# A transformer block on one core: the second MLP product copies its first results and adds the residual on GpSimd

## The chip, the cores and the metric

One core of a Trainium2 chip. Its engines run side by side, each with its own queue: TensorE (PE, matrix products, results in PSUM banks), VectorE (DVE), ScalarE (ACT), GpSimd (POOL) and SyncE (SP), which here only issues DMAs. The metric is the device time of one execution in microseconds (us). Before the change: 2175.38 us, the median of 3 runs (2174.56 to 2177.39).

## The reference

In float32, 2048 tokens of 1024 values, 32 heads of 32, 3584 hidden values:

```
h  = x + attention(layernorm(x)) @ wo            # 4 segments of 512 tokens with a running memory
y  = layernorm(layernorm(h))
g  = gelu(y @ w1 + b1)                           # 2048 x 3584
h2 = h + (g @ w2 + b2)                           # 2048 x 1024, the output
```

## The kernel before

Every float32 product is made of three matmuls: each operand is split into a rounded high half and a low half that holds the rest (ACT casts the high half, DVE or GpSimd subtracts to get the low one), and high x high, high x low, low x high are summed in one bank.

The program runs over two halves of 1024 tokens. A half has attention (16 units of a head group and a segment, a table of steps gives the order), the product with `wo`, and the first MLP product in 14 pairs of column blocks (`Mixer.pair`), which makes `gelu` and stores it to DRAM (`h_dram`). Near the end of half 0, beside the last nine pairs, `ln1` normalises the next half's tokens: `ln_transpose` (L156) turns 128 x 128 blocks on PE into a bank of the tags it is given, ACT and DVE take them out as halves. The pairs take their own banks by tags: `bps` from `d` (three banks), `dps` from `pt` (two). The tags `qk` (two) belong to attention's scores.

After half 1 comes the second MLP product, class `Second`, by Strassen's seven products in Winograd's form. `Second` runs 112 jobs, two rounds (s = 0 and 1, one for each half of the hidden values) of 56. A round goes through the product names 1, 7, 6, 5, 3, 2, 4; a job is a name and a pair p of token tiles p and p + 8 (8 pairs); 1 alternates with 7, 6 with 5, 3 with 2. A job is 21 matmuls: 7 blocks of 128 by three. In round 1, job 56 is the first, job 70 is (7, pair 6), job 72 is (6, pair 0), job 73 (6, pair 1), job 75 (6, pair 2). What stands around a job n is in `work(n)`, called after the matmuls of n are written down, and each engine runs its part in that order:

- `rows_ahead`, `load_rows` (L1264): SP loads rows of `w2` or stored sums of them (`w2r`, four buffers) a few jobs ahead
- `load_items` (L1311, L1308): SP loads items, 128 x 896 tiles of `gelu` (`hr`), into one of six buffers, first freed, first used, up to six jobs ahead, and no further than buffers are free
- `sums` (L1331 to L1344): GpSimd combines items. For name 6 the sum of L1336 and L1337 needs three items; the second sum is also stored to DRAM (`s2_dram`, L1402) in the next job's `work`, to be loaded again for name 3
- `prep` (L1357, L1358): ACT casts and DVE subtracts the item of job n + 2. It stands two jobs ahead of its use, on three buffers in turn. When it is done the item's buffer is free again
- `add` (L1428): DVE adds the bank to one or two of the 32 output tiles `c` (128 x 512, all kept in SBUF)
- `fill` (L1275, L1283, L1284): GpSimd pre-sums two rows of `w2`, ACT and DVE make halves of them
- `ahead`: `out` gives a home to the output tiles that the next two jobs need and loads the residual `h` + b2 into them from `h1_dram` (L1372), so that every `add` adds to the residual. The 32 loads lie between the end of the pairs and job 13

SP issues in the written order; a load that waits for its buffer holds all behind it. At most eight of SP's DMAs are under way: each has one of eight queue semaphores in turn and waits for the DMA that had it before.

## Time and profile before

| | us |
|---|---|
| median of 3 runs | 2175.38 |
| profiled execution, its time | 2176.5 |
| profiled execution, its span | 2174.8 |
| PE busy in the span | 2154.5 |
| DVE, ACT, POOL busy | 1357.8, 1100.5, 950.1 |
| second MLP product: from about 1636 to the end, PE busy there | 532.99 of 538.80 |

Rows of the profile name line, engine, operation and tile. In the list of waits a row gives the engine and its line, what ended the wait, the sum, the number and the longest. In a timeline a row gives start, length, engine, line, operation, and in brackets the idle time before it and what ended that. A group's row ends in count, busy us, mean ns, and the idle time before. A DMA row ends in count, size and the median us from issue to landing. GB/s and the DMA share are of 16 engines. The granted TensorE clock was 1.00 throughout the second product but for its last slice (0.98).

### The profile page before, as it was taken

How to read it: one execution, taken by the hardware profiler on the slowest of the kernel's cores; microseconds unless marked ns; L12 is line 12 of the kernel's file. 1: busy time of each engine (PE TensorE's matmuls, PEld its weight loads, DVE VectorE, ACT ScalarE, POOL GpSimd, SP SyncE). 2: the span in 40 equal slices, each digit the busy share in tenths (PEclk: the TensorE clock that was granted, in tenths of full speed). 3: DMA queues.
4: the chain of work that ended last, by engine and by line, in shares of the span. 5: the costliest groups of instructions: out<-in, count | busy, mean ns of one | idle time of the engine just before them, and what ended most of it. 6: DMA issues, size and time to landing. Idle time of an engine off the chain costs nothing.

```text
span 2174.8 us, 33225 instructions
## 1 busy us (share of the span) xinstructions
PE 2154.5 (99%) x10937; PEld 1750.0 (80%) x10937; DVE 1357.8 (62%) x2696; ACT 1100.5 (51%) x2433; POOL 950.1 (44%) x1206
## 2 busy tenths in 40 slices
PE   8999999999999999999999999999999999999999
PEld 6877777778888888877777778888888788888887
DVE  7766666655745656666667655745666665576753
ACT  5777777753543445777777753633343232322321
POOL 5533335461434434533335551534446544255340
PEclk9999999999999999999999999999999999999999
DMA  7444444664575555444444763576569865676762
GB/s 202 117 117 107 107 107 127 198 203 155 169 211 154 180 163 152 121 117 107 107 107 125 204 214 134 170 213 174 160 202 380 280 223 178 201 241 214 260 227 91
DMA packets 352405, 376.20 MB, mean 173 GB/s; under 512 B 27214, under 2 KB 244330, under 8 KB 352234
## 3 DMA queue, kind: packets, MB, share of 16 engines
q1 hardware_dynamic: 289306, 337.25, 51.3%
q10 hardware_dynamic: 62928, 36.84, 5.7%
q8 instruction: 87, 1.43, 0.3%
q14 instruction: 84, 0.69, 0.1%
HBM read 241.27 MB, written 82.38 MB: 149 GB/s over the span
## 4 chain that ended last, share of the span: by engine, by line
PE 95%; DVE 2%; ACT 1%; DMA 1%; POOL 1%; issue 0%; SPq 0%; ACTq 0%; DVEq 0%; POOLq 0%
PE po L1418 24%; PE bps L1021 11%; PE cps L1021 7%; PE dps L1021 7%; PE pst L620 4%; PE po L634 3%; PE pqk L570 3%; PE pwo L127 3%; PE vps L127 3%; PE pwo L129 3%; PE qps L127 3%; PE pwo L128 3%; PE kps L127 3%; PE qps L128 3%; PE qps L129 3%; PE vps L128 3%
## 5 line engine op out<-in xcount | busy, mean ns | idle before, releaser
L572 DVE CUSTOM_DVE_ANT_0 pqk<-pqk,mask 128x512 f32<-128x512 f32 (+2 forms) x384 | 216.9, 565 | 235.5 <-PE pqk L570 205.1
L574 ACT ACTIVATE junk<-pqk,mx 128x512 f32<-128x512 f32 (+2 forms) x384 | 225.1, 586 | 133.0 <-DVE mx L572 124.7
L627 POOL TENSOR_SCALAR_AFFINE_SELECT e<-e 128x128 f32<-128x128 f32 (+1 forms) x384 | 136.0, 357 | 259.0 <-ACT e L623 253.9
L700 POOL TENSOR_TENSOR wl<-wr,wh 128x256 fp32r<-128x256 f32 x268 | 200.6, 764 | 107.2 <-DVE wh L696 43.5
L623 ACT ACTIVATE e<-pst 128x384 f32<-128x384 f32 (+1 forms) x384 | 200.4, 528 | 67.4 <-PE pst L620 66.4
L1428 DVE TENSOR_TENSOR c<-c,po 128x512 f32<-128x512 f32 x160 | 105.4, 683 | 150.7 <-PE po L1418 143.4
L620 PE MATMUL pst<-qs,ks 104*128 104x512 f32 (+3 forms) x512 | 140.7, 318 | 2.2 <-ACT e L623 1.2
L570 PE MATMUL pqk<-ks,qs 96*128 96x512 f32 (+2 forms) x384 | 137.8, 359 | 0.9 <-ACT junk L574 0.6
L620 PEld LDWEIGHTS pst<-qs,ks 104*128 104x128 f32 x512 | 95.7, 188 | 36.1 <-ACT e L623 11.5
L1418 PE MATMUL po<-w2h,zh 128*128 128x512 f32 x378 | 121.0, 390 | 2.0 <-ACT zh L1357 1.6
L1275 POOL TENSOR_TENSOR w2r<-w2r 128x512 f32<-128x512 f32 x54 | 83.0, 1547 | 70.9 <-DMA w2r<-in_B_w 65.0
L127 PE MATMUL qps<-yh,wh 128*128 128x512 f32 x256 | 113.1, 442 | 0.0
L127 PE MATMUL kps<-yh,wh 128*128 128x512 f32 (+1 forms) x264 | 113.0, 428 | 0.0
L1021 PE MATMUL bps<-zh,sb 128*128 128x512 f32 x336 | 111.0, 391 | 0.0
L1021 PE MATMUL bps<-zh,sa 128*128 128x512 f32 x336 | 110.8, 390 | 0.0
L1134 POOL TENSOR_TENSOR s<-r 128x512 f32<-128x512 f32 x28 | 44.0, 1571 | 142.3 <-DVE sa L1150 84.8
L127 PE MATMUL vps<-yh,wh 128*128 128x512 f32 x256 | 105.0, 410 | 0.0
L1418 PE MATMUL po<-w2h,hl 128*128 128x512 f32 x322 | 103.1, 390 | 0.0
L128 PE MATMUL kps<-yl,wh 128*128 128x512 f32 (+1 forms) x264 | 102.4, 388 | 0.6 <-DVE yl L165 0.3
L129 PE MATMUL kps<-yh,wl 128*128 128x512 f32 (+1 forms) x264 | 101.8, 386 | 0.0
L128 PE MATMUL qps<-yl,wh 128*128 128x512 f32 x256 | 101.0, 395 | 0.0
L128 PE MATMUL vps<-yl,wh 128*128 128x512 f32 x256 | 100.9, 394 | 0.0
(271 smaller groups left out, 6206.7 us busy)
## 6 DMA issues: line engine op xcount, KB each, us to landing
hr<-h_dram SPq DMA_DIRECT2D x112, 448.0 KB, 5.5
w2r<-in_B_w SPq DMA_DIRECT2D x122, 256.0 KB, 4.6
r<-in_B_w SPq DMA_DIRECT2D x56, 512.0 KB, 4.3
ks<-kk SPq DMA_DIRECT2D x360, 64.0 KB, 2.0
qs<-qq SPq DMA_DIRECT2D x360, 64.0 KB, 2.0
h_dram<-ht ACTq DMA_DIRECT2D x83, 256.0 KB, 3.8
wx<-in_B_w SPq DMA_DIRECT2D x56, 256.0 KB, 3.7
o_dram<-side SPq DMA_DIRECT2D x52, 256.0 KB, 4.3
```

Source lines behind the costliest of these rows:

```text
L127: nc.tensor.matmul(ps, ah, bh, start=first, stop=False)
L128: nc.tensor.matmul(ps, ah, bl, start=False, stop=False)
L129: acts["mm"] = nc.tensor.matmul(ps, al, bh, start=False, stop=last)
L570: nc.tensor.matmul(ps, u["qs"][0:96, j, i * P:(i + 1) * P], u["ks"][0:96, j, 0:n], start=True, stop=True)
L572: nc.vector.tensor_tensor_reduce(out=ps, in0=ps, in1=mask[:, 512 - n:512], op0=ALU.add, op1=ALU.min, scale=-SCALE, scalar=3.0e38, accum_out=m)
L574: at(now[0] + 1, lambda: nc.scalar.activation(acts["junk"][:, :n], ps, AF.Exp, bias=m, scale=-1.0, accum_out=u["mx"][:, 1, i, j:j + 1]))
L620: nc.tensor.matmul(ps[:, o:o + 512 - P * jk], u["ks"][:, j, jk * P:(jk + 1) * P], u["qs"][:, j, jk * P:512], start=True, stop=True)
L623: nc.scalar.activation(e, ps[:, :w], AF.Exp, scale=SCALE)
L627: nc.gpsimd.affine_select(d, d, pattern=[[0, 2], [1, P]] if n == 2 else [[1, P]], compare_op=ALU.is_ge, fill=0.0, base=0, channel_multipli ...
L700: nc.gpsimd.tensor_tensor(l[:, c], wr[:, c], raw(h)[:, c], op=ALU.subtract)
L1021: nc.tensor.matmul(ps, x_[:, c, :], y_[:, c, :], start=first and c == 0 and n == 0, stop=last and c == 3 and n == 2, skip_group_check=True)
L1418: nc.tensor.matmul(ps, x_[:, k], y_[k], start=opens and k == 0 and i == 0, stop=closes and k == self.KP - 1 and i == 2, skip_group_check=True)
```

## The change

1. `add`: the first product that meets an output tile is copied into it (`tensor_copy`); later ones are added as before. The residual loads between the end of the pairs and job 13, `ahead` and `NEED` are gone.
2. `residual`, in jobs 34 to 67 (`LATE`): each job loads one residual tile into a buffer that is lent by the item loads, and in the next job GpSimd adds it to its output tile. `plan` gives every output tile a job in which no product is added to it for six jobs. Two of the six item buffers are lent, from job 32 on, and given back at job 68.
3. `prep` and `work`: the buffer of a sum that has yet to be stored is free only when the store has been written down (`cool`).
4. `ln1(1, 0)` beside the pairs takes its banks from the tag `qk` alone, and no more from `av`, `pt`, `pt`.
5. The load of `wv` for the next head group stands at step 13 of a unit and no more at 18 (units 2, 3, 12, 13, 14 of each half).

```diff
@@ -211,7 +211,7 @@
         l = apool.tile([P, DC, 512], F32R, tag=f"al{n}", name=f"{what}l{n}")
         return h, l
 
-    def ln1(half, sl, delay=0, aside=None, gap=1):
+    def ln1(half, sl, delay=0, aside=None, gap=1, tags=("av", "pt", "pt")):
         xs = []
         for t in range(4):
             xt = lnp.tile([P, D], F32, tag="ln", name="xt", bufs=4)
@@ -227,7 +227,7 @@
             return acts["y", sl]
 
         yield from ln_tiles(lnp, xs, None, None, False, act=True, aside=aside, gap=gap,
-                            fold=lambda src, t4: ln_transpose(src, *home(), t4, ("av", "pt", "pt"), slow=True))
+                            fold=lambda src, t4: ln_transpose(src, *home(), t4, tags, slow=True))
 
     def opening():
 
@@ -725,7 +725,7 @@
             b = 24 * n
             if n < 15 and ORDER[n + 1][0] != g:
                 g1 = ORDER[n + 1][0]
-                for name, m, m1 in (("k", 2, 9 if n > 1 else 11), ("q", 7, 17), ("v", 18 if n > 1 else 11, 25)) if n else \
+                for name, m, m1 in (("k", 2, 9 if n > 1 else 11), ("q", 7, 17), ("v", 13 if n > 1 else 11, 25)) if n else \
                         (("k", 4 if half else 14, 19), ("q", 8 if half else 17, 24), ("v", 20, 34)):
                     if name != "v" or not early:
                         at(b + m, partial(wload, g1, name))
@@ -1238,6 +1238,8 @@
             self.free = list(range(6))
             self.part, self.later = [], []
             self.c, self.np, self.came = {}, 0, {}
+            self.adds, self.lent, self.saving, self.cool = [], [], [], []
+            self.plan()
 
 
         def slot(self, q):
@@ -1358,7 +1360,10 @@
                 getattr(nc, lower).tensor_tensor(l, src, raw(h), op=ALU.subtract)
                 self.hl[n] = [x.rearrange("p (k n) -> p k n", n=P) for x in (h, l)]
                 if (s, name, p, "21") not in self.raws:
-                    self.free.append(b)
+                    if name == "6" and any(x is src for _, x in self.later + self.saving):
+                        self.cool.append((src, b))
+                    else:
+                        self.free.append(b)
 
 
         HOMES = [("sp", "c", 4)] * 4 + [("cx", "c", 3)] * 3 + [("cl", "r", 4)] * 4 + [("mq", "p1", 3)] * 3 + \
@@ -1369,28 +1374,49 @@
                 pool, tag, bufs = self.HOMES[len(self.c)]
                 pool = self.mq if pool == "mq" else acts[pool]
                 self.c[t, c] = pool.tile([P, 512], F32, tag=tag, name="c", bufs=bufs)
-                nc.sync.dma_start(self.c[t, c], h1_dram[t][:, c * 512:(c + 1) * 512])
             return self.c[t, c]
 
-        NEED = {"1": ("11", "12"), "7": ("21", "22")}
         ADDS = {"1": ("11", "12"), "7": ("21", "22"), "6": ("21",), "5": ("12", "22"), "3": ("12",), "2": ("11",), "4": ("21",)}
+        LATE = (34, 68)
         LAST = {"5": "22", "3": "12", "2": "11", "4": "21"}
 
         def at(self, p, w):
             return p + self.PAIRS * (int(w[0]) - 1), int(w[1]) - 1
 
-        def ahead(self, n):
-
-            for m in (n + 1, n + 2):
-                if m < len(self.jobs) and self.jobs[m][0] == 0:
-                    _, name, p = self.jobs[m]
-                    for w in self.NEED.get(name, ()):
-                        self.out(*self.at(p, w))
+        def plan(self):
+
+            uses = {}
+            for n, (s, name, p) in enumerate(self.jobs):
+                for w in self.ADDS[name]:
+                    uses.setdefault(self.at(p, w), []).append(n)
+            self.rest, left = {}, sorted(uses, key=lambda k: uses[k][-1])
+            for n in range(*self.LATE):
+                free = [k for k in left if uses[k][0] < n and uses[k][-1] > n + 8 and not any(n <= m < n + 6 for m in uses[k])]
+                if free:
+                    self.rest[n] = free[0]
+                    left.remove(free[0])
+            assert not left
+
+        def residual(self, n):
+
+            for o, k in self.adds:
+                nc.gpsimd.tensor_tensor(o, o, k, op=ALU.add)
+            self.adds = []
+            if n in self.rest:
+                (t, c), b = self.rest[n], self.lent[n % 2]
+                k = acts["sp"].tile([P, self.KP * P], F32, tag=f"hr{b}", name="hr", bufs=1)[:, 0:512]
+                nc.sync.dma_start(k, h1_dram[t][:, c * 512:(c + 1) * 512])
+                self.adds = [(self.c[t, c], k)]
+            if n == self.LATE[1]:
+                self.free += self.lent
+                self.lent = []
 
         def work(self, n, got):
 
-            late, self.later = self.later, []
+            self.saving, self.later = self.later, []
             self.rows_ahead(n)
+            while self.LATE[0] - 3 < n < self.LATE[1] and len(self.lent) < 2 and self.free:
+                self.lent.append(self.free.pop())
             self.load_items(n)
             self.sums(n, n + 2)
             self.prep(n + 2)
@@ -1398,9 +1424,12 @@
             self.fill_up(n)
             self.sums(n, n + 4)
             self.rows_ahead(n)
-            for d, t in late:
+            for d, t in self.saving:
                 nc.sync.dma_start(d, t)
-            self.ahead(n)
+            self.free += [b for t, b in self.cool if any(t is x for _, x in self.saving)]
+            self.cool = [k for k in self.cool if not any(k[0] is x for _, x in self.saving)]
+            self.saving = []
+            self.residual(n)
 
         def product(self, n):
             s, name, p = self.jobs[n]
@@ -1424,8 +1453,12 @@
         def add(self, s, name, p, ps):
             for w in self.ADDS[name]:
                 t, c = self.at(p, w)
-                o = self.out(t, c)
-                nc.vector.tensor_tensor(o, o, ps, op=ALU.subtract if name == "4" else ALU.add)
+                if (t, c) in self.c:
+                    o = self.c[t, c]
+                    nc.vector.tensor_tensor(o, o, ps, op=ALU.subtract if name == "4" else ALU.add)
+                else:
+                    o = self.out(t, c)
+                    nc.vector.tensor_copy(o, ps)
                 if s == 1 and w in self.LAST.get(name, ""):
                     self.later.append((out[0, t * P:(t + 1) * P, c * 512:(c + 1) * 512], o))
 
@@ -1518,7 +1551,7 @@
                     pass
             acts["ahead"] = ln1(1, 1, gap=2)
             interleave(chain(*(mixer.pair(j) for j in range(HP - 9, HP))),
-                       chain(ln1(1, 0, 2), islice(acts["ahead"], 3)), 0.17)
+                       chain(ln1(1, 0, 2, tags=("qk",)), islice(acts["ahead"], 3)), 0.17)
             mp.release()
             mq.release()
             zx.release()
@@ -1545,8 +1578,6 @@
                         second.prep(n - 8, "gpsimd")
                     if (j, n) == (HP - 1, 9):
                         second.sums(0, 2)
-                    if (j, n) == (HP - 1, 12):
-                        second.ahead(-1)
             second.prep(2)
             wp.release()
             acts["cl"] = cl = tc.alloc_tile_pool(name="cl", bufs=1, reuse_waits="tile")
```

Where it moves instructions, three places are of weight. SP at jobs 68 to 73, with the items of the second round's name 6 (h_dram01 and h_dram11 are their sources; three loads make a pair's sum, w2r are weight rows). Before, from pair 1's first item on (19540, 19571, 19573); pair 0's three were loaded ahead of these rows (19464, 19466, 19505), and s2_dram0 stores its sum:

```order
L1311 DMA hr_19540<-h_dram01_152 128x896
L1311 DMA hr_19571<-h_dram11_154 128x896
L1311 DMA hr_19573<-h_dram01_152 128x896
L1402 DMA s2_dram0_80<-hr_19505 128x896
L1311 DMA hr_19602<-h_dram01_152 128x896
L1264 DMA w2r_19624<-in_B_w2 128x512 x2
L1264 DMA w2r_19627<-in_B_w2 128x512 x2
L1264 DMA w2r_19630<-in_B_w2 128x512 x2
L1311 DMA hr_19654<-h_dram11_154 128x896
L1311 DMA hr_19656<-h_dram01_152 128x896
L1264 DMA w2r_19669<-in_B_w2 128x512
L1402 DMA s2_dram1_81<-hr_19573 128x896
```

Now, from pair 1's items on (19631, 19633, 19661); pair 0's third item, 19629, is the row ahead of them:

```order
L1313 DMA hr_19631<-h_dram01_152 128x896
L1313 DMA hr_19633<-h_dram11_154 128x896
L1313 DMA hr_19661<-h_dram01_152 128x896
L1266 DMA w2r_19683<-in_B_w2 128x512 x2
L1266 DMA w2r_19686<-in_B_w2 128x512 x2
L1266 DMA w2r_19689<-in_B_w2 128x512 x2
L1313 DMA hr_19713<-h_dram01_152 128x896
L1266 DMA w2r_19728<-in_B_w2 128x512
L1428 DMA s2_dram0_80<-hr_19629 128x896
L1266 DMA w2r_19753<-in_B_w2 128x512
L1313 DMA hr_19755<-h_dram11_154 128x896
L1313 DMA hr_19757<-h_dram01_152 128x896
```

Pair 2's third item is 19656 before and 19757 now. The load of 19757 is into the buffer of 19629, behind the store of it, and waits for that store; the store itself, once ahead of the three weight rows, now stands behind them and behind one more weight load.

GpSimd at the same place (L1336, L1337 are L1338, L1339 now; L1275 is L1277). Before:

```order
L1336 TENSOR_TENSOR hr_19464<-hr_19464,hr_19466 128x896
L1337 TENSOR_TENSOR hr_19505<-hr_19464,hr_19505 128x896
L1275 TENSOR_TENSOR w2r_19496<-w2r_19496 128x512
L1275 TENSOR_TENSOR w2r_19499<-w2r_19499 128x512
L1275 TENSOR_TENSOR w2r_19502<-w2r_19502 128x512
L1336 TENSOR_TENSOR hr_19540<-hr_19540,hr_19571 128x896
L1337 TENSOR_TENSOR hr_19573<-hr_19540,hr_19573 128x896
L1275 TENSOR_TENSOR w2r_19537<-w2r_19537 128x512
L1275 TENSOR_TENSOR w2r_19624<-w2r_19624 128x512
L1275 TENSOR_TENSOR w2r_19627<-w2r_19627 128x512
L1275 TENSOR_TENSOR w2r_19630<-w2r_19630 128x512
```

Now:

```order
L1403 TENSOR_TENSOR c_17709<-c_17709,hr_19502 128x512
L1277 TENSOR_TENSOR w2r_19450<-w2r_19450 128x512
L1333 TENSOR_TENSOR hr_19525<-hr_19489,hr_19525 128x896
L1338 TENSOR_TENSOR hr_19564<-hr_19564,hr_19600 128x896
L1339 TENSOR_TENSOR hr_19629<-hr_19564,hr_19629 128x896
L1277 TENSOR_TENSOR w2r_19555<-w2r_19555 128x512
L1277 TENSOR_TENSOR w2r_19558<-w2r_19558 128x512
L1277 TENSOR_TENSOR w2r_19561<-w2r_19561 128x512
L1338 TENSOR_TENSOR hr_19631<-hr_19631,hr_19633 128x896
L1339 TENSOR_TENSOR hr_19661<-hr_19631,hr_19661 128x896
L1277 TENSOR_TENSOR w2r_19597<-w2r_19597 128x512
```

The sums of pairs 0 and 1 and the pre-sums of weights stand in the same order as before; two residual adds now go ahead of them. What is not the same is when SP loads their items: pair 0's first two in jobs 67 and 68, once both in 66, its third in 69, once in 67.

GpSimd in jobs 51 to 54, before:

```order
L1275 TENSOR_TENSOR w2r_18895<-w2r_18895 128x512
L1275 TENSOR_TENSOR w2r_18936<-w2r_18936 128x512
L1275 TENSOR_TENSOR w2r_18973<-w2r_18973 128x512
L1331 TENSOR_TENSOR hr_18922<-hr_18920,hr_18922 128x896
L1275 TENSOR_TENSOR w2r_18976<-w2r_18976 128x512
L1331 TENSOR_TENSOR hr_19001<-hr_18961,hr_19001 128x896
```

Now:

```order
L1277 TENSOR_TENSOR w2r_18905<-w2r_18905 128x512
L1403 TENSOR_TENSOR c_17335<-c_17335,hr_18951 128x512
L1277 TENSOR_TENSOR w2r_18947<-w2r_18947 128x512
L1403 TENSOR_TENSOR c_17477<-c_17477,hr_18994 128x512
L1277 TENSOR_TENSOR w2r_18987<-w2r_18987 128x512
L1333 TENSOR_TENSOR hr_19018<-hr_18975,hr_19018 128x896
L1403 TENSOR_TENSOR c_17408<-c_17408,hr_19031 128x512
L1277 TENSOR_TENSOR w2r_18990<-w2r_18990 128x512
L1403 TENSOR_TENSOR c_17554<-c_17554,hr_19067 128x512
L1333 TENSOR_TENSOR hr_19091<-hr_19055,hr_19091 128x896
```

Between two pre-sums there is now the add of a residual tile (L1403) that SP loaded at the end of the job before, behind that job's weight rows.

## The prediction, made before the changed kernel was run

> **What bounds the kernel now.** First the page's busy times, then the list of what TensorE (PE) waited for.

> ```profile
> PE 2154.5 (99%) x10937; PEld 1750.0 (80%) x10937; DVE 1357.8 (62%) x2696; ACT 1100.5 (51%) x2433; POOL 950.1 (44%) x1206
> PE pt L281 <- ACT xt L271: 8.6, 2, 8.2
> PE po L1418 <- ACT zh L1357: 1.6, 1, 1.6
> PE dps L1021 <- DVE ht L1046: 0.9, 1, 0.9
> PE po L1418 <- DVE zh L1358: 0.4, 1, 0.4
> PE pst L620 <- ACT e L623: 1.2, 3, 0.7
> ```

> PE is busy for 2154.5 of 2174.8 us. Of the rest, 8.6 us are the opening transposes, which the diff does not touch. What it can touch is 0.9 us in the pairs and 1.6 + 0.4 = 2.0 us in the second product. So an edit here can win about 2.9 us, and can lose as much as it makes PE wait: everything is read as "what is ready how long before PE wants it".

> The chain of waits shows how the 2.0 us came about (start, length in us):

> ```profile
> 1713.63 6.08 DMA hr<-h_dram
> 1719.71 1.27 POOL w2r L1275
> 1720.99 2.53 POOL hr L1336
> ...
> 1726.06 0.95 ACT zh L1357
> ...
> 1727.03 1.10 DVE zh L1358
> ```

> This is job 19: item loads on SyncE's queue (SP), a pre-sum and two sums on GpSimd (the second left out here), the cast, the subtraction. Job 75 is the same place of the second round. Two stretches by engine show what differs (PE, PEld, DVE, ACT, POOL, clock, DMA share, GB/s):

> ```profile
> 1640.00:1690.00 50.00, 49.97 (x221) 41.08 (x221) 35.91 (x41) 15.47 (x20) 28.98 (x15) 1.00 1.03 378
> 1850.00:1900.00 50.00, 50.00 (x223) 41.40 (x222) 26.96 (x32) 16.64 (x23) 10.38 (x7) 1.00 0.62 193
> ```

> The 32 residual loads of 256 KB (8.4 MB) sit in the stretch where the DMA engines are full.

> **The gains.** The copy in place of the add leaves DVE the same number of instructions on the same bank, behind the same product; it lies beside PE: 0. Without residual loads, job 19's chain should look like job 75's, which had no wait at all: I take -2.0 us (bounds -2.0 and 0, since weight rows and sums remain). In the pairs the transposes leave the two `pt` banks that `dps` turns in; the two `qk` banks are not used by anything else there. Its wait was for the bank behind L1046: -0.9 (bounds -0.9 and 0). The earlier `wv` load puts 512 KB ahead of the query copies on SP; no wait on a weight is in the list of waits, and the attention's own there are 0.7 at most (the row of L620): 0 (bounds -0.5 and +0.5). Sum of gains: -2.9.

> **The first cost: GpSimd's queue before the second round.** The 32 residuals now pass SP and GpSimd in jobs 34 to 65, one each. In order, the add of job n waits for a load that SP issues at the end of job n-1, behind that job's weight rows, and GpSimd's next pre-sum stands behind the add. Around job 52 nothing is left to spare (from the timelines of SP, POOL, ACT and DVE):

> ```profile
> 1890.93 5.44 SPq L1264 DMA_DIRECT2D w2r<-in_B_w  x4
> 1896.94 1.29 POOL L1275 TENSOR_TENSOR w2r<-w2r 128x512 f32<-128x512 f32 x1 [2.94 <-DMA w2r<-in_B_w]
> 1898.27 0.62 ACT L1283 CAST w2h<-w2r 128x512 fp32r<-128x512 f32 x1 [2.77 <-POOL w2r L1275]
> 1898.79 0.94 ACT L1357 CAST zl<-hr 128x896 fp32r<-128x896 f32 x1
> 1900.80 2.17 DVE L1358 TENSOR_TENSOR zl<-hr,zl 128x896 fp32r<-128x896 f32 x1
> 1970.65 0.39 PE L1418 MATMUL po<-w2h,zh 128*128 128x512 f32 x1
> 1975.41 0.39 PE L1418 MATMUL po<-w2h,zl 128*128 128x512 f32 x1
> w2r<-in_B_w SPq DMA_DIRECT2D x17, 256.0 KB, 3.5
> hr<-h_dram SPq DMA_DIRECT2D x11, 448.0 KB, 5.3
> ```

> PE's operands change at 1970.65 and 1975.41, the starts of jobs 70 and 71: a job is 4.76 us, so job 56 started at 1970.65 - 14 x 4.76 = 1904.0, and its third matmul, the first that reads the low half, 0.45 later. In the changed kernel the residual load stands behind the four weight loads: issued at 1890.93 + 5.44 + 0.4 = 1896.8. The last two rows are the DMA issues of 1868 to 1912, with their median to landing: 3.5 for 256 KB, 5.3 for the larger item, so it lands at 1900.3 to 1902.1. The add is not in this trace; the nearest row is the pre-sum of the same shape, 1.29 here and 1.57 in the table below: 1901.6 to 1903.7. Then the pre-sum that stood at 1896.94: to 1902.9 to 1905.2; cast 0.62; job 56's cast 0.94; its subtraction between 1.08 and 2.17: ready at 1905.6 to 1909, wanted at 1904.5. Cost 1.1 to 4.5; as jobs 55 to 57 move together I take 2.5 for them, and 0 as the low bound, if the load lands much sooner.

> **The second cost: a buffer that is still being stored.** Until job 68 two of the six item buffers are lent to the residuals, so the items of jobs 72 and on are loaded up to two jobs later. The rows of before:

> ```profile
> 1964.20 2.18 DVE L1358 TENSOR_TENSOR zh<-hr,zh 128x896 fp32r<-128x896 f32 x1
> 1967.31 0.37 SPq L1402 DMA_DIRECT2D s_dram<-hr  x1
> 1983.23 0.33 SPq L1264 DMA_DIRECT2D w2r<-in_B_w  x1
> 1988.23 2.41 POOL L1336 TENSOR_TENSOR hr<-hr 128x896 f32<-128x896 f32 x1 [0.95 <-DMA hr<-h_dram]
> 1993.84 1.09 DVE L1358 TENSOR_TENSOR hl<-hr,hl 128x896 fp32r<-128x896 f32 x1 [5.18 <-ACT hl L1357]
> L1337 POOL TENSOR_TENSOR hr<-hr 128x896 f32<-128x896 f32 x5 | 10.9, 2187 | 5.0 <-DMA hr<-h_dram 4.7
> L1275 POOL TENSOR_TENSOR w2r<-w2r 128x512 f32<-128x512 f32 x7 | 10.9, 1569 | 4.2 <-DMA w2r<-in_B_w 4.2
> L1336 POOL TENSOR_TENSOR hr<-hr 128x896 f32<-128x896 f32 x4 | 9.9, 2474 | 14.9 <-DMA hr<-h_dram 14.9
> hr<-h_dram SPq DMA_DIRECT2D x12, 448.0 KB, 5.9
> s_dram<-hr SPq DMA_DIRECT2D x4, 448.0 KB, 6.6
> ```

> Job 75 starts at 1970.65 + 5 x 4.76 = 1994.45; its low half is ready at 1993.84 + 1.09 = 1994.93, wanted at 1994.9. It was exactly in time; any delay is PE's. The sum at 1988.23 is pair 2's first; the store at 1967.31 is that of pair 0's sum, long done by then.

> In the changed order pair 0's sums stand behind the last residual add, pair 1's come behind three pre-sums, and pair 2's third item goes into the buffer of pair 0's sum, which SP must first store to DRAM. By the group means above (GpSimd, 1960 to 2010) and the medians (DMA issues, same stretch): pair 0's last item is issued at 1964.20 + 2.18 = 1966.4 (DVE reads its buffer until then) and lands 5.9 later, 1972.3; second sum to 1974.5; three pre-sums, 4.7, to 1979.2; pair 1's sums, 2.5 + 2.2, to 1983.9 (job 73's cast then ends at 1984.9, its start: nothing lost, or 1 us). The next pre-sum ends at 1985.5, cast 0.6, and DVE does job 73's subtraction, two adds and the weight subtraction by about 1988. That frees the row buffer for SP's weight load of 1983.23, and only behind it comes the store: 1988.4 instead of 1967.3. The store takes 6.6, to 1995.0; the load into the same buffer 0.4 + 5.9, to 2001.3; sum 2.2, cast 0.9, subtraction 1.1: 2005.5 against 1994.9, 10.6 us. With the quickest rows of these kinds,

> ```profile
> hr<-h_dram SPq DMA_DIRECT2D x3, 448.0 KB, 4.2
> s_dram<-hr SPq DMA_DIRECT2D x1, 448.0 KB, 5.7
> ```

> it is 1.7 + 0.9 less in the transfers and up to 2 less in GpSimd's three pre-sums and sums: 6.0. I take 8.5 (bounds 6 and 11): the wait of jobs 55 to 57 gives the loads some time that these sums do not count. From job 77 on all six buffers are back, a pair has 9.5 us and its chain takes no longer, so the loss is paid once.

> **The sum** against the profiled execution (2176.5, span 2174.8): -2.0 - 0.9 + 0 + 2.5 + 8.5 = +8.1, 2184.6. The median of the runs shown is 2175.4, 1.1 below the profiled one, so 2183.5. Its own range: from -2.9 - 0.5 + 0 + 6 = +2.6 to 0 + 0.5 + 4.5 + 11 = +16, so 2178 to 2191.

> **Rivals.** (1) The waits do not come, and the gains do: 2175.4 - 2.9 = 2172.5, not slower. Its one mechanism is job 75's store: if the load for pair 2 need not wait for it, or SP passes the weight load of 1983.23 at its old time, pair 2 is ready as before. For it: GpSimd stood idle 14.9 us before L1336 in that stretch, so there is room for sums in another place. Against: the changed program gives that load a wait on the store, and such waits are paid already, here two of up to 6.0 us (SP's waits, 1960 to 2010):

> ```profile
> SPq L1311 <- DMA s_dram<-hr: 11.8, 2, 6.0
> ```

> It decides from a store issued before about 1978: 12.9 us of store and load, 4.2 of sum, cast and subtraction end at 1994.9. (2) Only part of the delay is paid, 3 to 5 us, since the transfers find emptier queues: 2175.4 - 2.9 + 4 = 2176.5, not told from no change. For it: the DMA share is 0.62 there, not 1.03. (3) DVE becomes the bound before the second round, because GpSimd's adds hold up its two-input subtractions:

> ```profile
> 1900.00:1960.00 60.00, 60.00 (x266) 49.69 (x265) 45.47 (x46) 16.46 (x21) 30.43 (x17) 1.00 0.75 248
> 1953.57 2.12 POOL L1336 TENSOR_TENSOR hr<-hr 128x896 f32<-128x896 f32 x1 [5.18 <-DMA hr<-h_dram]
> 1953.62 3.02 DVE L1358 TENSOR_TENSOR zl<-hr,zl 128x896 fp32r<-128x896 f32 x1
> ```

> A subtraction of 1.08 took 3.02 beside a sum of 2.12 that began 0.05 before it. If each of the 12 adds from job 55 on costs DVE 1.57, it is busy 45.5 + 18.8 = 64.3 of 60 us: 4.3 more on top of the forecast, 2187.8. [...] (4) Job 19's wait stays, because GpSimd and not the DMA made it: 2185.5, inside the forecast's range; it is not counted apart.

> **How the numbers follow.** Forecast 0.62, rival 1 0.12, rival 2 0.18, rival 3 0.08. About 0.2% (4.4 us) can be told from no change here. All gains together are 2.9 + 0.5, under that, so faster gets 0.03. Slower by over 4.4: the forecast's part above +4.4, 0.55, and rival 3, 0.08: 0.63. The rest, 0.34, is no difference. The range 2174 to 2189 leaves out half of rival 1 and part of the highest cases.

> **What would show it.** Right: in the second product PE waits for the cast and subtraction of jobs 55 to 57 (1 to 4 us) and of job 75 (6 to 11), the load of pair 2's third item waits for the store of pair 0's sum, the store is issued some 20 us later than before; the wait of 0.9 at `dps` and the 2.0 at job 19 are gone. Wrong: if that load starts without a wait, if no wait over 1 us is left after job 19, or if DVE is busy throughout 1900 to 1960.

## The result, and the profile after

The changed kernel takes 2193.06 us (median of 6 runs, 2189.87 to 2193.66), the kernel before, on the same chip, 2175.77 (6 runs): ratio 1.0071, 95% interval 1.0061 to 1.0081. It is slower by 17.3 us, where +8.1 was forecast. The profiled execution took 2193.37 us, its span is 2191.3.

What PE waited for in the second product (view of waits, 1630 to 2190; line, releaser, us in total, times, longest):

```profile
PE po L1447 <- ACT hl L1359: 4.9, 1, 4.9
PE po L1447 <- ACT zh L1359: 3.2, 2, 3.1
PE po L1447 <- DVE c L1458: 1.7, 1, 1.7
PE po L1447 <- DVE zh L1360: 1.1, 3, 0.5
PE po L1447 <- DVE hl L1360: 0.8, 1, 0.8
PE po L1447 <- DVE zl L1360: 0.7, 1, 0.7
```

Before, this list held 1.6 and 0.4 us, at job 19. Those are down to 0.3 (one of the three `zh` waits), and the wait of 0.9 at `dps` is gone from the page. In their place stand 12.3 us in two groups, as PE's timeline shows (start, length, idle time before it in brackets; one wait of 0.16 us at job 73 is left out):

```profile
1900.48 0.50 PE L1447 MATMUL po<-w2h,zh 128*128 128x512 f32 x1 [3.05 <-ACT zh L1359]
1901.61 1.22 PE L1447 MATMUL po<-w2h,zh 128*128 128x512 f32 x2 [0.39 <-DVE zh L1360]
1908.84 0.73 PE L1447 MATMUL po<-zh,zl 128*128 128x512 f32 x2 [0.74 <-DVE zl L1360]
1914.72 0.50 PE L1447 MATMUL po<-zh,hl 128*128 128x512 f32 x1 [0.82 <-DVE hl L1360]
...
1992.12 0.73 PE L1447 MATMUL po<-w2h,zh 128*128 128x512 f32 x2 [0.48 <-DVE zh L1360]
1998.46 0.47 PE L1447 MATMUL po<-zh,zl 128*128 128x512 f32 x1 [1.74 <-DVE c L1458]
2008.38 0.80 PE L1447 MATMUL po<-w2h,hl 128*128 128x512 f32 x1 [4.89 <-ACT hl L1359]
```

These are jobs 55 to 57, which the prediction named, and jobs 73 to 75, of which it named job 75 (for job 73 it had "nothing lost, or 1 us"). But 12.3 us of waits, less the 1.7 won at job 19, are not 16.5, which is what the second product became longer by (first matmul of job 0 to the start of the last `add`: 536.5 us before, 553.0 after). Two stretches after the longest waits hold the rest (PE alone: stretch, length, PE busy, granted clock, DMA share, GB/s):

```profile
1897.84:1901.25 3.41, 0.73 (x2) 1.00 1.05 407
1901.25:1904.67 3.42, 3.06 (x7) 0.50 0.75 275
...
2003.64:2007.06 3.42, 0.00 (x0) 1.00 0.63 255
2007.06:2010.47 3.41, 2.08 (x4) 0.50 0.89 257
2010.47:2013.88 3.41, 3.41 (x9) 0.50 0.78 298
```

PE reads as busy there, so no list of waits shows it, but its granted clock is 0.50: 9 matmuls in the last stretch, where the job's pace at clock 1.00 (4.76 us for 21) would make 15. What that cost is estimated as half of the busy time at 0.50: 3.06 / 2 = 1.5 us in job 55, (2.08 + 3.41) / 2 = 2.75 us in job 75, which took 7.62 us, 2.86 over 4.76.

The whole account, from the starts of the first matmul of each job: what jobs took beyond 4.76 us. A wait ahead of a job's first matmul counts with the job before. (From start to start a wait took some 0.3 us more than its row says: the rows of the two groups sum to 5.0 and 7.3 us, the starts give 6.1 and 8.4, which stand in the column "waits".)

| jobs | before | after | of that, waits | of that, slow clock |
|---|---|---|---|---|
| 0, 1 | 0.3 | 0.3 | 0.3 | 0 |
| 18, 19 | 2.6 | 0.6 | 0.6 | 0 |
| 54 to 57 | 0 | 7.6 | 6.1 | 1.5 |
| 72 to 75 | 0.2 | 11.2 | 8.4 | 2.8 |
| all others | 0 | 0 | 0 | 0 |
| sum | 3.1 | 19.6 | 15.4 | 4.3 |

**How the second group arose** is in the chain of waits (start, length):

```profile
1987.43 2.45 POOL hr L1339
...
1993.26 1.77 DVE zl L1286
...
1995.04 0.33 SPq L1266
...
1995.41 3.91 DMA s_dram<-hr
...
1999.34 5.79 DMA hr<-h_dram
...
2005.29 2.08 POOL hr L1339
...
2007.39 0.95 ACT hl L1359
```

This is the forecast's second cost piece by piece: the sum on GpSimd, the weight subtraction on DVE that frees a row buffer, the weight load on SP, only behind it the store of pair 0's sum (issued at 1995.4, 28 us later than before, 22 against the start of job 70, which itself came 5.7 us later), then the load into the same buffer, the sum, the cast.

**The first group** grew in another way than forecast. Job 55's operand is late because its cast stands on ACT behind the cast of a pre-summed weight row, which came late from GpSimd:

```profile
1898.97 0.62 ACT L1285 CAST w2h<-w2r 128x512 fp32r<-128x512 f32 x1 [6.96 <-POOL w2r L1277]
```

GpSimd's pre-sums of weight rows, in the timelines before and after:

```profile
1871.90 1.43 POOL L1275 TENSOR_TENSOR w2r<-w2r 128x512 f32<-128x512 f32 x1 [18.36 <-DMA w2r<-in_B_w]
1877.67 2.02 POOL L1275 TENSOR_TENSOR w2r<-w2r 128x512 f32<-128x512 f32 x1 [4.34 <-DVE w2l L1284]
1885.18 1.29 POOL L1275 TENSOR_TENSOR w2r<-w2r 128x512 f32<-128x512 f32 x1 [5.48 <-DMA w2r<-in_B_w]
1892.71 1.28 POOL L1275 TENSOR_TENSOR w2r<-w2r 128x512 f32<-128x512 f32 x1 [6.25 <-DMA w2r<-in_B_w]
```

```profile
1872.97 1.29 POOL L1277 TENSOR_TENSOR w2r<-w2r 128x512 f32<-128x512 f32 x1
1880.12 1.29 POOL L1403 TENSOR_TENSOR c<-c,hr 128x512 f32<-128x512 f32 x1 [5.86 <-DMA hr<-h_dram]
1881.37 1.29 POOL L1277 TENSOR_TENSOR w2r<-w2r 128x512 f32<-128x512 f32 x1
1888.70 1.29 POOL L1277 TENSOR_TENSOR w2r<-w2r 128x512 f32<-128x512 f32 x1
1896.44 1.27 POOL L1403 TENSOR_TENSOR c<-c,hr 128x512 f32<-128x512 f32 x1 [6.46 <-DMA hr<-h_dram]
1897.68 1.26 POOL L1277 TENSOR_TENSOR w2r<-w2r 128x512 f32<-128x512 f32 x1
```

Job 54 started at 1894.49 before and at 1892.51 after, so 2.0 us are to be added to the times after. Then the four pre-sums are 3.1, 5.7, 5.5 and 7.0 us late. Each now stands behind a residual add, each add waited 4.4 to 6.5 us for its load, and each load stands on SP behind weight rows that wait for a row buffer. What they wait for is the store of an earlier pre-sum to DRAM (`t_dram`), as SP's waits from 1868 to 1905 show:

```profile
SPq L1266 <- DMA t_dram<-w2r: 13.8, 3, 5.4
```

So it is a ring: pre-sum, store, row buffer free, weight load, residual load, add, next pre-sum. In the same stretch of the kernel before SP waited 14.1 us for these stores, which speaks for a ring without slack already then. By 1881.37, in job 51, the ring was 5.7 us late. The prediction had priced the add ahead of one later pre-sum, that of 1896.94 (now at 1902.80, 7.8 us late).

### The profile page after: what moved, and what is told of

Same layout as the page of the kernel before. It is cut to its first block, busy times and chain, and to the rows that moved or that the text cites. A ratio compares the mean times of both kernels' runs of the same rounds, so it can differ in the third digit from the quotient of the medians.

```text
span 2191.3 us, 33246 instructions
## 1 busy us (share of the span) xinstructions
PE 2160.6 (99%) x10937; PEld 1752.5 (80%) x10937; DVE 1371.7 (63%) x2696; ACT 1101.4 (50%) x2433; POOL 1001.7 (46%) x1238
## 4 chain that ended last, share of the span: by engine, by line
PE 88%; POOL 3%; DMA 3%; issue 3%; DVE 2%; ACT 1%; SPq 0%; ACTq 0%; POOLq 0%; DVEq 0%
PE po L1447 17%; PE bps L1021 10%; PE cps L1021 7%; PE dps L1021 7%; PE pst L620 4%; PE po L634 3%; PE pqk L570 3%; PE kps L127 3%; PE pwo L127 3%; PE vps L127 3%; PE pwo L129 3%; PE pwo L128 3%; PE qps L127 3%; PE vps L128 3%; PE vps L129 3%
## 5 line engine op out<-in xcount | busy, mean ns | idle before, releaser
L623 ACT ACTIVATE e<-pst 128x384 f32<-128x384 f32 (+1 forms) x384 | 200.4, 528 | 67.9 <-PE pst L620 66.0
L1458 DVE TENSOR_TENSOR c<-c,po 128x512 f32<-128x512 f32 x128 | 84.9, 683 | 138.6 <-PE po L1447 138.5
L620 PE MATMUL pst<-qs,ks 104*128 104x512 f32 (+3 forms) x512 | 140.6, 317 | 1.5 <-ACT e L623 1.0
L620 PEld LDWEIGHTS pst<-qs,ks 104*128 104x128 f32 x512 | 95.7, 188 | 35.2 <-ACT e L623 10.9
L1021 PE MATMUL bps<-zh,sb 128*128 128x512 f32 x336 | 111.0, 391 | 0.0
L1021 PE MATMUL bps<-zh,sa 128*128 128x512 f32 x336 | 110.8, 390 | 0.0
L129 PE MATMUL qps<-yh,wl 128*128 128x512 f32 x256 | 100.7, 393 | 0.0
## 6 DMA issues: line engine op xcount, KB each, us to landing
hr<-h_dram SPq DMA_DIRECT2D x112, 448.0 KB, 5.0
w2r<-in_B_w SPq DMA_DIRECT2D x122, 256.0 KB, 4.5
h_dram<-ht ACTq DMA_DIRECT2D x83, 256.0 KB, 3.7
wx<-in_B_w SPq DMA_DIRECT2D x56, 256.0 KB, 3.5
o_dram<-side SPq DMA_DIRECT2D x52, 256.0 KB, 4.4
```

Source lines behind the costliest of these rows:

```text
L129: acts["mm"] = nc.tensor.matmul(ps, al, bh, start=False, stop=last)
L620: nc.tensor.matmul(ps[:, o:o + 512 - P * jk], u["ks"][:, j, jk * P:(jk + 1) * P], u["qs"][:, j, jk * P:512], start=True, stop=True)
L623: nc.scalar.activation(e, ps[:, :w], AF.Exp, scale=SCALE)
L1021: nc.tensor.matmul(ps, x_[:, c, :], y_[:, c, :], start=first and c == 0 and n == 0, stop=last and c == 3 and n == 2, skip_group_check=True)
```

## Which part costs what: residuals and lent buffers taken away

**Lending alone.** The residual loads and adds are left out, the two buffers are still withheld.

```diff
-            if n in self.rest:
-                (t, c), b = self.rest[n], self.lent[n % 2]
-                k = acts["sp"].tile(...)[:, 0:512]
-                nc.sync.dma_start(k, h1_dram[t][:, c * 512:(c + 1) * 512])
-                self.adds = [(self.c[t, c], k)]
```

> The changed kernel without any residual (32 loads and 32 adds left out, so the output lacks the residual), but with two item buffers withheld from job 32 to job 68 as before. Theory (two separate costs: the adds on GpSimd's queue make jobs 55 to 57 wait, the missing buffers make jobs 73 to 75 wait): the first cost goes (5.0 us of waits and 1.8 of slow clock), the second stays at least in part, 7.3 + 2.9 us: about 2186, with a wait of 3 to 5 us ahead of job 75. Rival (the residual adds behind which the sums stand make both): no wait over 1 us is left, 2173.

Measured: 2183.55 us against 2177.05, ratio 1.0032 (1.0021 to 1.0043). PE's waits in the second product:

```profile
PE po L1442 <- ACT hl L1359: 4.4, 1, 4.4
PE po L1442 <- DVE c L1453: 1.7, 1, 1.7
```

Jobs 54 to 57 take 4.76 us each, jobs 73 to 75 together 9.4 us more (10.8 in the changed kernel), with 6.8 us of clock 0.50 from 1998.4. So the two costs are separate, and the second comes from the missing buffers, without a single residual add.

**Neither residuals nor lending.** The same lines are left out, and the one that fills `self.lent`:

```diff
-            while self.LATE[0] - 3 < n < self.LATE[1] and len(self.lent) < 2 and self.free:
-                self.lent.append(self.free.pop())
```

> The changed kernel without any residual and without the lending (loads and adds left out, so the output lacks the residual; all six item buffers stay with the items). Both theories: what is left of the change is its gains. Predicted: job 19's 2.0 us and the 0.9 us in the pairs, 2175.8 - 2.9 = 2172.9. If the copied product itself, or the transposes in the score banks, cost something, it is above 2174.

Measured: 2174.72 us against 2177.05, ratio 0.9989 (0.9980 to 0.9998). No wait over 0.4 us is left in the second product. The gains are there: 2.3 us of the 2.9 expected, and all of the loss lies in the residuals' new way.

**Buffers back at job 60,** six residuals left out:

```diff
-            if n in self.rest:
+            if n in self.rest and n < 60:
...
-            if n == self.LATE[1]:
+            if n == 60:
```

> The changed kernel without the six residuals of jobs 60 to 65 (their loads and adds are left out, so six output tiles lack the residual); the two lent buffers go back at job 60, not 68. Theory (job 75's wait comes from the buffers that come back too late, so that pair 2's item has to wait for a store): the waits ahead of jobs 73 to 75 go (0.64 + 1.74 + 4.89 us) and with them the slow clock of job 75 (2.9), while those of jobs 55 to 57 stay: 2193.1 - 10.2 = 2182.9. Rival (the second round's group of three items is late because of all that GpSimd and the queues were given before it, not because of the buffers): part of the waits at 73 to 75 stays, 2186 to 2193.

Measured: 2181.05 against 2176.38, ratio 1.0024 (1.0012 to 1.0035). Jobs 73 to 75 take 4.76, 4.76 and 4.78 us, jobs 54 to 57 still 7.2 us too much. Against the kernel before, the loss falls from 17.3 to 4.7 us, 2.4 more than the 10.2 expected; the waits of the first group are 0.6 shorter here and the slow clock lasts as long, so most of that difference isn't explained by the trace.

## The ring: adds in other jobs

**Two stretches** hold all 32 adds, and the buffers are lent for these alone:

```diff
-        LATE = (34, 68)
+        LATE = ((34, 50), (84, 100))
```

> The changed kernel with the same 32 residual adds in other jobs: 16 in jobs 34 to 49, 16 in jobs 84 to 99, the two buffers lent for these two stretches alone. Nothing is left out. Theory (the adds cost only where GpSimd's queue or the item buffers have nothing to spare, at jobs 50 to 59 and 68 to 77): neither of the two costs comes, the gains of 2.9 us stay, 2172.9 (ratio 0.9987). Rival (the second window has no room either: sums or weight pre-sums of jobs 88 to 99 come late): a wait of 1 to 5 us there, 2174 to 2179.

Measured: 2182.32 against 2177.05, ratio 1.0032 (1.0019 to 1.0046). A miss: the second group is gone but for 0.7 us at job 75, yet jobs 55 to 57 still take 4.7 us too much, though the last add of the first stretch is that of job 50. GpSimd's timeline:

```profile
1886.77 1.29 POOL L1403 TENSOR_TENSOR c<-c,hr 128x512 f32<-128x512 f32 x1 [5.04 <-DMA hr<-h_dram]
1888.01 1.30 POOL L1277 TENSOR_TENSOR w2r<-w2r 128x512 f32<-128x512 f32 x1
1892.59 1.69 POOL L1277 TENSOR_TENSOR w2r<-w2r 128x512 f32<-128x512 f32 x1 [3.28 <-DVE c L1458]
1899.66 1.30 POOL L1277 TENSOR_TENSOR w2r<-w2r 128x512 f32<-128x512 f32 x1 [5.38 <-DMA w2r<-in_B_w]
```

Job 54 starts 2.6 us earlier in this run than before, so the pre-sums of 1888.01 and 1899.66 are 5.4 and 5.3 us late against 1885.18 and 1896.94 of before: what the adds of jobs 48 to 50 cost the ring is still missing at 1899.66, 12 us after the last of them. (The pre-sum between, that of 1892.59, is only 2.5 us late, so it isn't one constant shift.) PE's waits of 0.92 and 2.45 us at 1902.50 and 1905.68 come of it.

**The first stretch ends at job 45:**

```diff
-        LATE = ((34, 50), (84, 100))
+        LATE = ((29, 46), (84, 99))
```

> As the version with two stretches, but 17 adds in jobs 29 to 45 and 15 in jobs 84 to 98; nothing is left out. With adds up to job 50 the waits ahead of jobs 56 and 57 had stayed (0.9 + 2.4 + 0.4 us), though no add stood on GpSimd's queue after 1888. Theory (each residual load and add of jobs 47 to 50 lengthens the ring weight load, residual load, add, pre-sum, cast, subtraction, row buffer free, next weight load, whose turns were 5.8 to 7.5 us before and 7.4 to 8.3 with the adds, and the delay adds up until job 56): with the adds out of jobs 46 to 52 these waits are as without residuals, 0.4 us. Rival (the two buffers lent until then make the items of jobs 50 to 56 late): they went back four jobs earlier, too, but with the buffers lent and no adds no wait was left there, so this is held unlikely. Time: 2177.1 + 0.4 - 2.9, about 2174.5, if the second stretch still costs the 1.4 us that it cost at jobs 90 and 91.

Measured: 2177.61 against 2175.71, ratio 1.0006 (0.9997 to 1.0015). Jobs 54 to 57 and 72 to 75 take 4.76 us each; so ending the stretch four jobs earlier removes the whole first group. The two buffers went back four jobs earlier as well; that they alone made the waits is unlikely, since with the buffers lent to job 68 and no residuals jobs 54 to 57 took 4.76 us. No run has the residual loads without the adds, so which of the two delays the ring isn't parted. The time was expected 2.6 us under that of the kernel before and is 1.9 above it. Of these 4.5 us the trace explains 1.4: 0.7 at job 35, and 2.1 in place of 1.4 at jobs 90 and 91. (The version below without adds in jobs 84 to 91 has no wait there.)

## SyncE's order

**Stores first.** In `work`:

```diff
             self.saving, self.later = self.later, []
+            for d, t in self.saving:
+                nc.sync.dma_start(d, t)
+            (the two lines on self.cool, and self.saving = [])
             self.rows_ahead(n)
...
-            for d, t in self.saving:
-                nc.sync.dma_start(d, t)
```

> The changed kernel with the stores of a job (pairs' sums to DRAM, output tiles) issued at the start of the next job's work, ahead of its weight rows and item loads, not behind them. Theory (the store of pair 0's sum stood behind a weight load that waited for a row buffer until 1995.0, though the sum was there at 1989.9): it goes out some 5 us earlier, the wait of 4.89 us ahead of job 75 is gone or under 1 us, and with it that job's slow clock: 2193.1 - 4.9 - 2.9, about 2185.3. Rival (something behind the store, the load's own place on the queue or GpSimd's, makes pair 2 late anyway): less than 2 us is won, 2191 to 2193.

Measured: 2190.07 against 2176.38, ratio 1.0069 (1.0054 to 1.0084): as the changed kernel, 1.0071. A miss. PE now waits 1.2 and 2.2 us at job 75, but jobs 72 to 75 still take 11.2 us too much in the profiled execution (2195.43 us, the longest of the four). SP's queue says why:

```profile
1997.43 0.42 SPq L1418 DMA_DIRECT2D s_dram<-hr  x1
1998.75 0.33 SPq L1266 DMA_DIRECT2D w2r<-in_B_w  x1
1999.13 3.57 SPq L1313 DMA_DIRECT2D hr<-h_dram  x3
```

The store of pair 0's sum left at 1991.96, 5.5 us earlier against the jobs, but the load that was to profit stands behind the next weight load, which waited for its row buffer until 1998.75, as late against the jobs as in the changed kernel (there at 1996.74). So pair 2's last item landed only 2.6 us earlier against the jobs, and this didn't reach PE either: the subtraction for job 75 ran from 2007.83 for 2.92 us, beside a sum on GpSimd from 2007.70 for 2.09 (1.09 us in the changed kernel), and the slow clock stayed, for 6.83 us.

**Stores and item loads first.** Beside that:

```diff
+            self.load_items(n)
             self.rows_ahead(n)
...
-            self.load_items(n)
             self.sums(n, n + 2)
```

> The run with the stores moved ahead won little: pair 2's last load then left SyncE's queue at 1999.1, right behind a weight load that had waited for its row buffer until 1998.8. Here a job's stores and then its item loads are issued ahead of its weight rows. Theory (it is the place on SyncE's queue behind weight loads that makes pair 2 late, for its store and for its load): both go out when their buffers allow, the waits at job 75 (1.2 and 2.2 us with the stores moved) and its slow clock are gone or under 1 us, about 2190.1 - 3.5 - 3.2 = 2183.4. Rival (a load into the buffer that is being stored now holds up the queue itself, some 6 us, and the weight rows behind it): the waits move to the weight rows of jobs 72 to 80, less than 2 us is won, 2188 to 2191.

Measured: 2186.84 against 2175.71, ratio 1.0054 (1.0041 to 1.0068), between the two expectations. Job 75's wait is gone (4.78 us), but job 74 now waits 3.6 us (none before, 1.7 in the changed kernel), and jobs 72 to 75 take 5.8 us too much in place of 11.2. About half of the second cost goes with the place on SP's queue: 2.8 us of it are the slow clock, which the shorter waits no longer bring (1.00 throughout), the rest are waits. The other half went only where the buffers came back earlier or were never lent.

## The clock

**PE kept busy in the two long waits,** by matmuls into the unused bank:

```diff
+            for i in range({55: 12, 75: 20}.get(n, 0)):
+                if i == 0:
+                    spare = bank("spare", "av", 1)
+                nc.tensor.matmul(spare, self.before[0][:, i % self.KP], self.before[1][i % self.KP], start=True, stop=True, ...)
+            self.before = ah, bh
```

> The changed kernel with matmuls of no use in front of the two long waits: 12 ahead of job 55 and 20 ahead of job 75, with the operands of the job before, into the one PSUM bank that the second product does not use. At 0.227 us each they fill 2.7 of the 3.05 us and 4.5 of the 4.9 us for which PE waited there. Theory (after a long wait PE runs at a lower granted clock, and that cost 1.8 us in job 55 and 2.9 us in job 75): the jobs come at 0.227 us a matmul again, no slice shows a clock under 0.95, and the time falls by 4.7 us, from 2193.1 to about 2188.4. Rival (the matmuls there are slow for another reason, such as the transfers and the sums that run beside them): jobs 55 and 75 stay at 7.0 and 7.6 us, the time at 2193.

Measured: 2189.89 against 2176.38, ratio 1.0062 (1.0047 to 1.0077). The clock stays at 1.00 where it was 0.50:

```profile
1900.00:1904.00 4.00, 3.93 (x18) 1.00 0.70 266
2006.00:2010.00 4.00, 4.00 (x19) 1.00 0.94 308
```

Job 55 falls from 7.00 to 5.12 us, job 75 from 7.62 to 4.96. Useless work in a wait makes these two jobs 4.5 us shorter, with the same transfers beside them, so their slowness was the clock. 1.4 us of it come back at job 56, whose operand is no earlier (wait 2.2 in place of 0.7), and the time falls by 3 to 4 us, not by 4.7.

**Which waits lower the clock?** In the kernel before, PE was made to wait by casts on ScalarE at the end of `work`:

```diff
+            k = {33: 1, 37: 2, 41: 3, 45: 4, 89: 5, 93: 6, 97: 7, 101: 8, 105: 4, 108: 3}.get(n, 0)
+            if k:
+                h0, h1 = self.used, self.hl[n + 1][0]
+                for _ in range(k):
+                    nc.scalar.copy(h0[:, 0:4], raw(h1)[:, 0:4])
+                nc.scalar.copy(h1[:, 0:1], raw(h1)[:, 0:1])
```

> The kernel before, with PE made to wait ahead of ten jobs of the second product by a chain on ScalarE that begins when the job before has ended: k casts of 128x512 (0.62 us each) and one short one. k is 1, 2, 3, 4 ahead of jobs 34, 38, 42, 46, then 5, 6, 7, 8 ahead of jobs 90, 94, 98, 102, then 4 and 3 ahead of jobs 106 and 109. Waits of about 1.0, 1.6, 2.2, 2.9, 3.5, 4.1, 4.7, 5.3, 2.9 and 2.2 us, 30 in all. Theory (a wait of 3 us or more lowers the granted clock for some 5 us behind it, one of 1.7 us and less does not): the job behind a wait of up to 2.2 us takes 4.76 us without the wait, behind one of 3.5 and more 6.5 to 7.7; in all 2175.8 + 30 + 4 x 2.5, about 2216, more if 2.9 is long enough. Rival (the slow matmuls belong to the place, not to the wait): 4.76 us behind all ten, 2206.

Measured: 2193.93 us. The waits were shorter than meant, since the casts began after the job's twelfth matmul, 9 before its end (they write only columns of the operand's first four blocks): none above 0.3 us for up to three casts, then 0.8, 1.4, 2.1, 2.7 and 3.4 us for four to eight. The wait of 2.1 us lowered the clock and that of 2.7 did not:

```profile
2087.67:2091.08 3.41, 1.38 (x6) 1.00 0.54 212
2091.08:2094.50 3.42, 3.42 (x10) 0.50 0.20 35
...
2111.56:2114.97 3.41, 1.60 (x7) 1.00 0.66 211
```

Neither theory had that: the length of these waits doesn't decide. The clock fell 1.4 us after the shorter wait had ended, and the two slow stretches of this run lasted 3.4 and 6.8 us.

**Waits of two lengths at eleven places,** the same edit of the kernel before with other jobs:

```diff
-            k = {33: 1, 37: 2, 41: 3, 45: 4, 89: 5, 93: 6, 97: 7, 101: 8, 105: 4, 108: 3}.get(n, 0)
+            k = {33: 7, 36: 6, 39: 7, 42: 6, 89: 6, 92: 7, 95: 6, 98: 7, 101: 6, 104: 7, 107: 6}.get(n, 0)
```

> The kernel before with waits of two lengths, about 2.2 and 2.9 us from the end of one job's matmuls to the next job's (six and seven casts in the chain), ahead of eleven jobs: 34, 37, 40, 43 and 90 to 108 in steps of three. Behind the waits of before the granted clock fell to 0.50 for 3.4 or 6.8 us, and the edges of these stretches in one run lie on multiples of 3.413 us from each other (2091.1 and 2135.5: 44.4 = 13.0 x 3.413; 1901.25 and 2007.05 in the changed kernel: 105.8 = 31.0 x 3.413). Theory (the clock is set at the edges of a fixed grid of 3.413 us, by how long PE was idle since the last edge; 1.8 us was not enough, 2.0 was): whether a wait lowers the clock depends on where it lies on the grid, so that waits of one length differ: of the long ones about two in three do, of the short ones about one in two, and each edge of a slow stretch lies on one grid. Rival (the length of the wait decides, between 2.2 and 2.9 us or elsewhere): all waits of one length do the same.

Measured: 2212.46 us. Four slow stretches, with their first edges at 1729.00, 1804.10, 2101.06 and 2118.12 (from slices of 0.1 us): 75.10, 296.96 and 17.06 us apart, which are 22.0, 87.0 and 5.0 times 3.413 (389.12 us in all, 114 times 3.4133). In slots of that length, counted from these edges, PE's busy time and the clock (0.50 behind the slots that end at the four edges):

```profile
1725.59:1729.00 3.41, 1.74 (x7) 1.00 0.94 310
1800.68:1804.10 3.42, 0.73 (x4) 1.00 1.02 326
1838.23:1841.64 3.41, 1.99 (x9) 1.00 0.03 8
2080.57:2083.98 3.41, 1.57 (x7) 1.00 1.01 363
2097.64:2101.06 3.42, 1.34 (x6) 1.00 0.78 275
2101.06:2104.47 3.41, 3.41 (x10) 0.50 0.52 167
2114.71:2118.12 3.41, 1.33 (x7) 1.00 0.75 296
```

Waits of one length do differ: of the five of 2.7 us two lowered the clock, of the six of 2.1 us one did. The wait of 2.73 us at 1839.65 is the clearest: it lies half in one slot and half in the next, the two hold 2.10 and 1.99 us of work, and the clock stays at 1.00. Of the slots looked at in this run, the one before and the changed kernel, those of 3.41 us at clock 1.00 with 1.38 us of work or less were followed by clock 0.50 each time (7 slots), those with 1.77 or more never. Between them four slots stand, 1.57, 1.60 and 1.69 without and 1.74 (two pauses, at job 19) with a slow stretch, so the border isn't sharp in these numbers. In the run with stores and item loads first, the wait of 3.6 us at job 74 left the clock at 1.00 in each us from 1990 to 2006. The number of waits that would fall was guessed too high (2 in 3 and 1 in 2).

## The edits in the pairs, and a version meant to beat both

**The pairs' edits alone,** in the kernel before:

```diff
-("v", 18 if n > 1 else 11, 25)
+("v", 13 if n > 1 else 11, 25)
...
-chain(ln1(1, 0, 2), islice(acts["ahead"], 3)), 0.17)
+chain(ln1(1, 0, 2, tags=("qk",)), islice(acts["ahead"], 3)), 0.17)
```

> The kernel before with the edits in the pairs alone: the transposes of the second half's first layer norm take the two score banks, and the value weights are loaded 5 steps earlier. Predicted: the wait of 0.9 us of the pairs' products is gone and nothing else changes, 2175.8 - 0.9 = 2174.9 (ratio 0.9996). Rival (the earlier value weights hold up the queue, or the score banks make other transposes wait): 2175.8 to 2177.

Measured: 2175.15 against 2177.05, ratio 0.9992 (0.9983 to 1.0001). The wait at `dps` is gone from the list. The time is 1.9 us less, with an interval from 3.7 less to 0.2 more, so that both 0.9 and nothing lie in it. Job 19's waits came to 0.50 and 0.40 us in this execution, with all residual loads in place.

**Mixed.** 8 residuals loaded as in the kernel before, 24 added in other jobs:

```diff
-        LATE = (34, 68)
+        LATE = ((30, 46), (92, 100))
...
+        def ahead(self, n):
+            for m in (n + 1, n + 2):
+                if m < 4:
+                    _, name, p = self.jobs[m]
+                    for w in self.ADDS[name]:
+                        t, c = self.at(p, w)
+                        if (t, c) not in self.c:
+                            nc.sync.dma_start(self.out(t, c), h1_dram[t][:, c * 512:(c + 1) * 512])
```

> A version meant to be faster than both: 8 residuals loaded ahead as in the kernel before (those of jobs 0 to 3, 2 MB in place of 8.4), 24 added by GpSimd, in jobs 30 to 45 and 92 to 99. Nothing is left out. Theory: the DMA engines have room again before job 19, no add stands in jobs 46 to 52 or 84 to 91, the two buffers are never missing where three items are loaded: only the short waits of the version without residuals are left, 2177.1 - 2.5, about 2174.5 (ratio 0.9988). Rival (2 MB ahead, beside the weights and the items of jobs 0 to 8, still makes job 19 wait): 2176 to 2177, no difference.

Measured: 2175.71 (11 runs, 2172.65 to 2179.47) against 2175.71, ratio 1.0000 (0.9991 to 1.0008). In the profiled execution, the quickest of the 11, every job but 19 and 35 takes 4.76 us within 0.15, those two 0.2 and 0.7 more, and the span is 2170.8. So both costs and job 19's wait are gone from the trace, and still the median isn't lower. Where the other executions lose what this one wins was not found; it is not faster by anything that could be measured. One part may be that the kernel before loses less in most executions than in the profiled one: what it waits for at job 19 changes (next section).

## Why the prediction was wrong

- **Gains, -2.0 and -0.9: the waits went, the sizes are not shown.** Job 19's excess fell by 2.0 us against the profile before. But that wait is not the same in each execution: up to job 33 the two runs with casts on ScalarE are the kernel before, and at job 19 one waits 1.27 and 0.40 us, the other 0.39 alone, where the profile before had 1.57 and 0.39. So 2.0 was one execution's wait taken for the kernel's, and that it came out is in part luck. The wait at `dps` went, too. The 0.9 doesn't show in the profiled execution, whose opening ran 1.5 us later (the transposes of L161 begin at 33.28, before at 31.77).
- **The copy in place of the add, 0: right** as far as the trace shows: without residuals the kernel is faster than before.
- **The second cost, +8.5 (bounds 6 and 11): right in mechanism and size.** Its waits came to 8.4 - 0.2 us, some 3 of them already at jobs 73 and 74, where at most 1 was forecast. The chain runs through the store as forecast, though two errors offset each other: the store left SP 1.4 us later against the jobs than worked out, and took 3.9 us, not 5.7 to 6.6. Moving the store alone showed that the item load's own place on SP was an equal link, which the working had not seen.
- **The first cost, +2.5 (bounds 0 and 4.5): right place, too small.** The waits cost 6.1 us, more than its upper bound. The failed step is "around job 52 nothing is left to spare": it priced one add, and took everything ahead of it to run as before. But the residuals of jobs 48 and 49 had already delayed the ring of weight loads, pre-sums and row buffers by 5.7 us, and so job 55 waited, one pre-sum ahead of the one that was priced.
- **The sum: a term was missing.** "A loss is as much as it makes PE wait" left out the clock. It cost 1.5 us after the wait of 3.05 and 2.8 after that of 4.89, 4.3 in all. Either miss alone, 4.3 or the 3.6 of the first cost, would have left the time inside the range that ends at 2189; together they did not. Of the 8.8 us between the forecast's +8.1 and the profiled +16.9, 4.3 are the clock, 3.6 the first cost, 0.9 the gain that the opening hid; the second cost's -0.3 and 0.3 outside the span cancel.
- **The rivals.** Waits that don't come, or come to 3 to 5 us, fell with the 12.3 us. DVE as the bound fell too; where it is busiest it still has room:

```profile
1930.00:1960.00 30.00, 30.00 (x134) 24.82 (x134) 24.88 (x27) 8.56 (x11) 28.61 (x16) 1.00 0.82 278
```

DVE is busy for 24.9 of 30 us there, and PE for all 30. That each add would cost DVE its whole 1.57 us was an estimate from one pair of rows. The full engine is GpSimd, with 28.6.

## What to carry to other kernels

A wait of PE had two prices here, its length and the clock behind it: by the clock column an estimated 1.5 us more after the wait of 3.05 us and 2.75 after that of 4.89, where PE had worked 0.73 us and not at all in the 3.41 us ahead of the drop to 0.50. Look for it in the clock column, not in the list of waits. When an operation is put into an in-order queue, follow the ring that this queue belongs to (load, sum, cast, buffer free, next load) from the first such operation: here a delay of 5.3 us of the ring still stood 12 us after the last of them. The two lent buffers cost where they came back late: 9.4 us at jobs 73 to 75 in the run that lends them to job 68 without residuals, 0.02 us there in the run that gives them back at job 60. So it is worth asking which jobs reload a lent resource first, before asking what the borrower does with it.
